# Attention, soft mixture of experts and Mish layer on one core: loads for the last layer moved into rooms that the experts' first weights leave, and one more room

## The chip, the cores and the metric

The kernel runs on one core of one Trainium2 chip (trn2). The metric is the device time of one execution in microseconds. The kernel before takes 679.25 us (median of 3 runs, 678.71 to 683.32).

## The reference, cut to what matters

Three stages follow each other. Attention with rotary positions gives 2304 tokens of 512 features. A soft mixture of 8 experts with 4 slots each mixes the tokens into 32 slots, runs each expert's two weight matrices on its slots, and mixes the results back. The last layer multiplies by `w_in`, applies Mish and multiplies by `w_out`.

```
logits = x @ phi                                  # 2304 x 32
d = softmax of logits over the tokens
slot_input = d.T @ x                              # 32 slots x 512
h = relu(slot_input[e] @ w1[e])                   # 8 experts: 512 -> 1024
slot_out[e] = h @ w2[e]                           # 1024 -> 512
c = softmax of logits over the slots
x = c @ slot_out
h = x @ w_in                                      # 512 -> 2048
g = h * tanh(log1p(exp(h)))                       # Mish
out = g @ w_out                                   # 2048 -> 512
```

## The kernel before, in words

**Attention** (L720 to L746) runs over pairs of heads and takes the first 395 us. Beside it `w_in` is converted and written to a scratch tensor `scr_in` in the chip's memory, and the first expert weights are loaded.

**Rooms.** The experts' weights come in 32 halves of 1 MB (16 of `w1`, 16 of `w2`), each in a *room* of 128 x 2048 words. There are 23 rooms: 14 that are there from the start (5 in pool `ra`, 9 in pool `rd`), 3 in pool `rc` and NRB = 6 in pool `rb` (L768), which opens when attention's buffers are gone. `order` is the list of what still has to come: w1 halves, w2 halves, then four parts of `w_in`. When a half has been multiplied, `used` (L139) hands its room to the next half of the experts, if one is left, and issues its load. If none is left, the room is kept in the list `rooms` when it is one of `ra`. The last four halves of w2 come as 16 quarters of 256 KB.

**Experts.** The first matrices are multiplied at L810 (tile `h_ps`), the second at L843 (`so_ps`). Between the four groups of the second, `combine` (L821) transposes the combine weights of one batch at a time into the tile `ct` (L831, L833).

**Last layer.** It works on units of 256 tokens by 256 hidden features: 72 units in 3 blocks of 24. These steps feed it:

- `load_out(c)` loads rows of `w_out` raw (512 KB) into one of four half-rooms, `outer(c)` makes of them two tiles, a rounded one (`wo_h`) and the rest (`wo_l`). ScalarE scales the raw words (L497, L498) and rounds (L896); VectorE does L503, L504, L505, L509, L510 and the subtraction L897. There are 16 of these, all in the first block.
- `inner(j)` folds the experts' result `s_t` into 256 columns of `w_in`: TensorE `m_wp` (L911), ScalarE copy `wp` (L913), TensorE `m_w` (L915), ScalarE cast L917, VectorE subtraction L918 into `wst`. There are 8, all in the first block.
- `mish(u)` multiplies `wst` with `ct` (TensorE `hp`, L932), ScalarE does Mish (`gg`, L938), a rounded copy `gh` (L940) and the rest `gl` on VectorE (L941). `second(u)` then does 12 matmuls `o_ps` (L957), four units behind.

**What sets the order.** All loads are issued by SyncE's queue in the order of the program; those marked by `keep_in_program_order` stay there. The instructions of TensorE, ScalarE and VectorE are put in order by a scheduler when the kernel is built; on the chip each engine takes its own list from the front. `s_t` (L857) is the experts' result, `so_ps` copied (L853), transposed (`m_sot`, L856) and copied again.

The raw half-rooms and the first two parts of `w_in` are taken from `rooms`, so from rooms of `ra` that the last w2 halves leave (L873 to L878):

```
for i in range(4):
    if i % 2:
        t = rooms[i][0].tile([128, 2048], U32, tag=rooms[i][1], name="raw")
        raws += [t[:, 0:1024], t[:, 1024:2048]]
    else:
        take(*rooms[i])
```

Of the kernel before, what the change touches and what calls it, by code (L numbers as in the profile page):

```python
# [42 lines left out]
def kernel(  # L43
# [13 lines left out]
    nc = tc.nc  # L57
# [6 lines left out]
    R = S - 512  # L64
    SCALE = 1.0 / float(D) ** 0.5
    KDM = DM // 128
    NRA, NRB, NRC = 8, 6, 3


    const = ctx.enter_context(tc.tile_pool(name="const", bufs=1))  # L70
# [22 lines left out]
    ring = ExitStack()  # L93
    ra = ring.enter_context(tc.tile_pool(name="ra", bufs=1, side="right"))
    late = ExitStack()
    rd = late.enter_context(tc.tile_pool(name="rd", bufs=1, side="right"))

    early = ExitStack()
    ae = early.enter_context(tc.tile_pool(name="ae", bufs=1, side="right"))
# [39 lines left out]
    def used(key):  # L139

        room = parts.pop(key)[1]
        if order[0][0] < 3:
            fetch(take(*room))
        elif room[0] is ra:
            rooms.append(room)

    rooms = []
# [612 lines left out]
    h_sb = p4.tile([128, F1], F32, name="h_sb")  # L760
    so_sb = si_t.rearrange("p c x -> p (c x)")[:, 0:DM]
    s_t = p2.tile([128, KDM, NSLOT], F32, name="s_t")
    ct = p2.tile([128, NT], F32R, name="ct")
    nc.gpsimd.memset(si_t, 0.0)
    for t in h_t:
        nc.gpsimd.memset(t, 0.0)
# [51 lines left out]
                used((1, 4 * eg + g, hf))  # L818
    tc.keep_in_program_order(nc.scalar.preload_act_table_set("mish"))

    def combine(b):  # L821

        for t0, nt in ((0, 4), (4, 1)):
            ps = ps_m.tile([128, nt, 128], F32, tag="m", name="m_ct")
            for j in range(nt):
                for o in range(0, 128, 32):
                    nc.tensor.matmul(ps[o:o + 32, j, :], lhsT=c_all[:, b, t0 + j], rhs=ident, start=True, stop=True)
            n = 512 if nt == 4 else R
            src = ps.rearrange("p t n -> p (t n)")[:, 0:n]
            dst = ct[:, b * S + t0 * 128:b * S + t0 * 128 + n]  # L830
            nc.scalar.copy(dst, src)  # L831
            for o in (32, 96):
                nc.vector.tensor_tensor(out=dst[o:o + 32], in0=src[o:o + 32], in1=dst[o:o + 32].bitcast(F32),  # L833
                                        op=ALU.subtract)

    so_ps = ps_m.tile([128, DM], F32, tag="m", name="so_ps")
    for eg in range(2):
# [25 lines left out]
    ps_p = ctx.enter_context(tc.tile_pool(name="ps_p", bufs=2, space=PSUM, reuse_waits="tile"))  # L863
    ps_o = ctx.enter_context(tc.tile_pool(name="ps_o", bufs=6, space=PSUM, reuse_waits="tile"))
    p3 = ctx.enter_context(tc.tile_pool(name="p3", bufs=1, reuse_waits="tile"))
    wo_h = [p3.tile([128, DM], F32R, name=f"wo_h{i}") for i in range(NFC)]
    wo_l = [p3.tile([128, DM], F32R, name=f"wo_l{i}") for i in range(NFC)]
    wst = p3.tile([128, F2], F32R, name="wst")
    p6 = ctx.enter_context(tc.tile_pool(name="p6", bufs=3, reuse_waits="tile"))


    raws = []
    for i in range(4):  # L873
        if i % 2:
            t = rooms[i][0].tile([128, 2048], U32, tag=rooms[i][1], name="raw")
            raws += [t[:, 0:1024], t[:, 1024:2048]]
        else:
            take(*rooms[i])  # L878
    for i in range(2):
        take(p3, f"wi{i}")  # L880

    def load_out(c):

# [4 lines left out]
    def outer(c):  # L888

        t = raws[c % 4]  # L890
        w = p6.tile([128, DM], F32, tag="w", name="w", bufs=2)
        sg = p6.tile([128, DM], U32, tag="sg", name="sg", bufs=2)
        scale_words(t)
        high_word(t, sg, w.bitcast(U32))
        low_word(nc.vector, t, sg, w)
        nc.scalar.copy(wo_h[c], w)  # L896
        nc.vector.tensor_tensor(out=wo_l[c], in0=w, in1=wo_h[c].bitcast(F32), op=ALU.subtract)  # L897

    for x in (0, "i0", 1, 2, 3, "i1"):
        if isinstance(x, int):  # L900
            load_out(x)
        else:
            fetch((3, int(x[1]), 0), behind=True)
# [23 lines left out]
    def mish(u):  # L927
        i, j = units[u]
        hp = ps_p.tile([128, 2, 256], F32, tag="p", name="hp")
        for x in range(2):  # L930
            f = 2 * j + x
            nc.tensor.matmul(hp[:, x, :], lhsT=wst[:, f * 128:(f + 1) * 128], rhs=ct[:, i * 256:(i + 1) * 256],  # L932
                             start=True, stop=True)
        hp = hp.rearrange("p a n -> p (a n)")
        gg = p6.tile([128, 512], F32, tag="gg", name="gg")
        gh = p6.tile([128, 512], F32R, tag="gh", name="gh", bufs=LOOK + 1)
        gl = p6.tile([128, 512], F32R, tag="gl", name="gl", bufs=LOOK + 1)
        nc.scalar.activation(out=gg, in_=hp, func=AF.Mish)  # L938

        (nc.scalar.copy if u < NG * GR else nc.vector.tensor_copy)(gh, gg)  # L940
        nc.vector.tensor_tensor(out=gl, in0=gg, in1=gh.bitcast(F32), op=ALU.subtract)  # L941
        gs[u] = gh, gl
# [3 lines left out]
    def second(u):  # L946
        i, j = units[u]
        gh, gl = gs.pop(u)
        for n in range(2):
# [3 lines left out]
            for x in range(2):  # L953
                f = 2 * j + x
                cols = slice(x * 256 + n * 128, x * 256 + n * 128 + 128)
                for k_, (g_, w_) in enumerate(((gh, wo_h), (gh, wo_l), (gl, wo_h))):
                    nc.tensor.matmul(ps, lhsT=g_[:, cols], rhs=w_[f], start=(j == 0 and x == 0 and k_ == 0),  # L957
                                     stop=(j == NG - 1 and x == 1 and k_ == 2))
            if j == NG - 1:
                ob = p6.tile([128, DM], F32, tag="ob", name="ob", bufs=3)  # L960
# [23 lines left out]
    for u in range(len(units) + LOOK):  # L984
        if u < len(units):
# [3 lines left out]
            if g == 0:  # L989
                if i < 2:  # L990
                    load_out(2 * j + 4 + i)
                if i == 0 and j % 2 == 0 and 2 + j // 2 < NFB:
                    fetch((3, 2 + j // 2, 0), behind=True)
                if j + 1 < NG:
                    if i < 2:
                        outer(2 * j + 2 + i)
                    if i == 1:
                        inner(j + 1)
# [53 lines left out]
```

## Time and profile before

| what | value |
|---|---|
| median of 3 runs | 679.25 us (678.71 to 683.32) |
| the profiled execution | 679.22 us |
| its span in the trace | 677.3 us |
| TensorE matmuls busy | 626.2 us, 92% of the span |
| VectorE, ScalarE, GpSimd busy | 404.9, 332.7, 206.8 us |
| data moved by DMA | 107.32 MB |
| mean granted TensorE clock | 0.982 |

Times in the trace are microseconds from the start of the span. The execution's own time is 1.9 us longer than the span. "Idle before" in a row is how long the engine did nothing ahead of that instruction, with what ended the wait. A busy TensorE row can overlap the next one, since matmuls are pipelined.

### The profile page before, as it was taken

Reading aid. Unit: us, or ns where it says so; the run is one execution under the profiler, and the core shown is the slowest. Engines: PE = TensorE matmul, PEld = TensorE weight load, DVE = VectorE, ACT = ScalarE, POOL = GpSimd, SP = SyncE. Lnnn points to the kernel's source line nnn. Section 1 sums busy time; section 2 is a strip of 40 time slices with the busy share of each in tenths; the row PEclk is TensorE's granted clock in tenths of the full one; section 3 lists DMA queues with packets and bytes.
Section 4 is the critical chain, followed back from the end, with each engine's and each line's share of the span. In section 5 each row is a group of like instructions: output and inputs, shape, how many; then the busy total and the mean of one; then the engine's idle time right before and its main releaser. Section 6 shows DMA issues by size and latency. Waiting matters only on the chain.

```text
span 677.3 us, 11071 instructions
## 1 busy us (share of the span) xinstructions
PE 626.2 (92%) x4002; PEld 461.1 (68%) x4002; DVE 404.9 (60%) x833; ACT 332.7 (49%) x755; POOL 206.8 (31%) x255
## 2 busy tenths in 40 slices
PE   1588899979999999999999998779999999999997
PEld 1565677657677777677677653357787888888885
DVE  6778677784775665656665421599973533343331
ACT  2556766763667656656565301288744321221221
POOL 5659759745675345424300010000000000000000
PEclk9999999998999999999999999969999999999999
DMA  9677689867596775346559579974300300030003
GB/s 265 158 208 186 190 263 270 205 219 199 157 291 183 189 215 130 90 112 172 129 181 315 185 267 379 339 266 164 125 1 0 94 1 0 1 94 0 1 0 94
DMA packets 58454, 107.32 MB, mean 158 GB/s; under 512 B 12704, under 2 KB 25120, under 8 KB 57888
## 3 DMA queue, kind: packets, MB, share of 16 engines
q1 hardware_dynamic: 58400, 106.62, 52.8%
q8 instruction: 32, 0.52, 0.4%
q14 instruction: 22, 0.18, 0.1%
HBM read 69.21 MB, written 8.91 MB: 115 GB/s over the span
## 4 chain that ended last, share of the span: by engine, by line
PE 77%; DMA 7%; DVE 5%; ACT 5%; SPq 2%; issue 2%; POOL 2%; ACTq 0%; DVEq 0%; POOLq 0%
PE o_ps L957 28%; PE m_av L426 14%; PE t L371 8%; PE s L330 5%; PE s L332 4%; PE s L350 3%; DMA w<-in_moe_w_in_dram 3%; PE hp L932 2%; PE so_ps L843 2%; DMA raw<-in_moe_w_out_dram 2%; PE m_lg L452 2%; SPq L185 1%; DMA w<-in_moe_w_dram 1%; PE tk L385 1%; ACT P L364 1%
## 5 line engine op out<-in xcount | busy, mean ns | idle before, releaser
L358 DVE TENSOR_REDUCE nmax<-s 128x1 f32<-128x576 f32 x144 | 108.2, 753 | 66.8 <-PE s L332 38.8
L364 ACT ACTIVATE P<-s,nmax 128x576 f32<-128x576 f32 x144 | 107.3, 745 | 28.2 <-DVE nmax L358 20.5
L957 PE MATMUL o_ps<-wo_h,gh 128*128 128x512 f32 x288 | 114.9, 399 | 0.8 <-ACT gh L940 0.8
L957 PE MATMUL o_ps<-wo_l,gh 128*128 128x512 f32 x288 | 113.9, 396 | 0.0
L957 PE MATMUL o_ps<-wo_h,gl 128*128 128x512 f32 x288 | 108.4, 391 | 0.0
L330 PE MATMUL s<-qk_st 128*128 128x288 f32 x256 | 85.6, 349 | 13.3 <-ACT P L364 7.8
L938 ACT ACTIVATE gg<-hp 128x512 f32<-128x512 f32 x72 | 42.3, 599 | 103.6 <-PE hp L932 100.9
L371 PE MATMUL t<-cs,P 128*128 128x128 f32 x512 | 79.5, 283 | 6.0 <-DVE partl L270 3.3
L407 ACT COPY PT<-t 128x512 f32<-128x512 f32 x93 | 54.2, 586 | 53.4 <-PE t L371 53.0
L371 PEld LDWEIGHTS t<-cs,P 128*128 128x128 f32 x512 | 59.9, 144 | 23.1 <-issue 11.6
L426 PE MATMUL m_av<-PT,w 128*64 128x320 f32 (+1 forms) x384 | 73.1, 421 | 0.9 <-ACT PT L396 0.6
L332 PE MATMUL s<-k_st,qk_st 128*128 128x288 f32 x256 | 73.4, 301 | 0.0
L330 PEld LDWEIGHTS s<-qk_st 128*128 128x128 f32 x256 | 49.7, 194 | 31.0 <-ACT P L364 11.5
L940 DVE CAST gh<-gg 128x512 fp32r<-128x512 f32 x48 | 20.5, 427 | 75.0 <-ACT gg L938 75.0
L228 POOL TENSOR_TENSOR w<-w,cs 128x512 f32<-128x512 f32 x34 | 45.6, 1343 | 61.9 <-PE m_k L282 53.6
L957 PEld LDWEIGHTS o_ps<-wo_h,gh 128*128 128x128 f32 x288 | 54.8, 190 | 13.8 <-ACT gh L940 2.9
L957 PEld LDWEIGHTS o_ps<-wo_h,gl 128*128 128x128 f32 x288 | 54.2, 188 | 11.7 <-DVE sg L509 0.4
L957 PEld LDWEIGHTS o_ps<-wo_l,gh 128*128 128x128 f32 x288 | 54.9, 191 | 9.3
L941 DVE TENSOR_TENSOR gl<-gg,gh 128x512 fp32r<-128x512 f32 x72 | 49.4, 690 | 8.9 <-ACT gh L940 4.4
L332 PEld LDWEIGHTS s<-k_st,qk_st 128*128 128x128 f32 x256 | 49.9, 195 | 0.0
L225 POOL TENSOR_TENSOR w<-w,cs 128x512 f32<-128x512 f32 x34 | 44.5, 1308 | 8.3 <-DMA w<-in_k_dram 3.8
L426 PEld LDWEIGHTS m_av<-PT,w 128*64 128x64 f32 x384 | 26.6, 136 | 22.2 <-issue 9.0
(172 smaller groups left out, 995.6 us busy)
## 6 DMA issues: line engine op xcount, KB each, us to landing
w<-in_moe_w_dram SPq DMA_DIRECT2D x28, 1024.0 KB, 7.6
w<-in_moe_w_in_dram SPq DMA_DIRECT2D x16, 512.0 KB, 6.8
raw<-in_moe_w_out_dram SPq DMA_DIRECT2D x16, 512.0 KB, 4.1
qk_st<-parth SPq DMA_DIRECT2D x46, 144.0 KB, 3.2
qk_st<-partl SPq DMA_DIRECT2D x46, 144.0 KB, 3.2
w<-in_q_dram SPq DMA_DIRECT2D x16, 256.0 KB, 5.5
w<-in_k_dram SPq DMA_DIRECT2D x16, 256.0 KB, 4.7
w<-in_moe_w_dram SPq DMA_DIRECT2D x16, 256.0 KB, 5.6
```

Of the source, the lines that this page charges most:

```text
L225: eng.tensor_tensor(out=tb, in0=src, in1=sin.to_broadcast([128, n, w]), op=ALU.mult)
L228: eng.tensor_tensor(out=dst, in0=sv, in1=cv, op=ALU.mult)
L330: nc.tensor.matmul(s[:, half, 0:288], lhsT=st[:, qc:qc + 128], rhs=st[:, KC + o:KC + o + 288], start=first, stop=False)
L332: nc.tensor.matmul(s[:, half, 0:288], lhsT=st[:, qc:qc + 128], rhs=k2_st[p % 2][:, o:o + 288], start=False, stop=last)
L358: nc.vector.tensor_reduce(out=stat[p][0][:, i:i + 1], in_=s[:, :, 0:288], axis=AX.XY, op=ALU.max, negate=True)
L364: nc.scalar.activation(out=P[p, t][:, h * S:(h + 1) * S].rearrange("p (a b) -> p a b", a=2), in_=s[:, :, 0:288], func=AF.Exp, bias=stat[p] ...
L371: nc.tensor.transpose(ps[:, j, :], P[p, t][:, blk * 128:(blk + 1) * 128], ident)
L407: nc.scalar.copy(dst, src)
L426: nc.tensor.matmul(ps[o:o + 64, :], lhsT=lhsT, rhs=rhs, start=(c == 0), stop=(c == 4))
L938: nc.scalar.activation(out=gg, in_=hp, func=AF.Mish)
L941: nc.vector.tensor_tensor(out=gl, in0=gg, in1=gh.bitcast(F32), op=ALU.subtract)
L957: nc.tensor.matmul(ps, lhsT=g_[:, cols], rhs=w_[f], start=(j == 0 and x == 0 and k_ == 0), stop=(j == NG - 1 and x == 1 and k_ == 2))
```

## The change

It adds one room to `rb` (NRB 6 to 7), so that 24 of the 32 halves have a room from the start and 8 are reloaded instead of 9. It keeps the rooms of `rd` too when no expert weight is left for them. The pool `rd` lives as long as `ra`. The rooms are given out anew, in the order in which they come free: first two for the raw rows of `w_out`, one for part 0 of `w_in`, one for 1792 of the 2304 columns of `ct`, then rooms for the tiles that were `wo_h` and `wo_l` (now `wo[c][0]` and `wo[c][1]`, four tiles in a room) and for parts 1 and 2 of `w_in`. Part 3 gets the room of part 0. `combine` cuts its writes where `ct` is cut. The order of the loads changes: two raw rows ahead of part 0 of `w_in`, and parts 2 and 3 are issued a little later.

```diff
-    NRA, NRB, NRC = 8, 6, 3
+    NRA, NRB, NRC = 8, 7, 3
...
-    rd = late.enter_context(tc.tile_pool(name="rd", bufs=1, side="right"))
+    rd = ring.enter_context(tc.tile_pool(name="rd", bufs=1, side="right"))
...
-        elif room[0] is ra:
+        elif room[0] in (ra, rd):
             rooms.append(room)
...
-    ct = p2.tile([128, NT], F32R, name="ct")
+    CTA = 1792
+    cts = [None, p2.tile([128, NT - CTA], F32R, name="ct1")]
...
+    rt = [room(U32) for _ in range(2)]
+    raws = [t[:, o:o + 1024] for t in rt for o in (0, 1024)]
+    take(*rooms.pop(0))
+    cts[0] = room(F32R)
+    wo = []
+    def wo_room():
+        t = room(F32R)
+        wo.extend((t[:, o:o + DM], t[:, o + DM:o + 2 * DM]) for o in (0, 2 * DM))
+    wo_room()
+    wo_room()
...
-            nc.scalar.copy(dst, src)
-            for o in (32, 96):
-                nc.vector.tensor_tensor(out=dst[o:o + 32], in0=src[o:o + 32], in1=dst[o:o + 32].bitcast(F32),
-                                        op=ALU.subtract)
+            a = b * S + t0 * 128
+            m = min(max(CTA - a, 0), n)
+            for x, y, t, w in ((0, m, 0, a), (m, n, 1, a - CTA)):
+                if x == y:
+                    continue
+                d = cts[t][:, w + x:w + y]
+                nc.scalar.copy(d, src[:, x:y])
+                for o in (32, 96):
+                    nc.vector.tensor_tensor(out=d[o:o + 32], in0=src[o:o + 32, x:y], in1=d[o:o + 32].bitcast(F32),
+                                            op=ALU.subtract)
...
-    wo_h = [p3.tile([128, DM], F32R, name=f"wo_h{i}") for i in range(NFC)]
-    wo_l = [p3.tile([128, DM], F32R, name=f"wo_l{i}") for i in range(NFC)]
...
+    wo_room()
+    take(*rooms.pop(0))
+    wo_room()
+    wo_room()
+    take(*rooms.pop(0))
+    for _ in range(3):
+        wo_room()
...
-    for x in (0, "i0", 1, 2, 3, "i1"):
+    for x in (0, 1, "i0", 2, 3, "i1"):
...
-                if i == 0 and j % 2 == 0 and 2 + j // 2 < NFB:
+                if i == 2 and j in (0, 2):
+                    if j:
+                        take(*parts[3, 0, 0][1])
                     fetch((3, 2 + j // 2, 0), behind=True)
```

On VectorE, from the copy of `s_t` to the first subtraction into `wst`, the kernel before has these rows (`raw` is a raw half-room, `w` and `sg` are work tiles of `outer`, L897 writes `wo_l`):

```order
L503 TENSOR_SCALAR sg<-raw 128x512
L504 SCALAR_TENSOR_TENSOR w<-raw,sg 128x512
L505 TENSOR_SCALAR sg<-w 128x512
L509 TENSOR_TENSOR sg<-sg,raw 128x512
L510 TENSOR_TENSOR w<-w,sg 128x512
L897 TENSOR_TENSOR wo_l_4859<-w,wo_h_4843 128x512
L503 TENSOR_SCALAR sg<-raw 128x512
L504 SCALAR_TENSOR_TENSOR w<-raw,sg 128x512
L503 TENSOR_SCALAR sg<-raw 128x512
L505 TENSOR_SCALAR sg<-w 128x512
L504 SCALAR_TENSOR_TENSOR w<-raw,sg 128x512
L918 TENSOR_TENSOR wst<-m_w,wst 64x256
```

In the changed kernel the same piece of VectorE's list has 15 rows; three of `outer(0)` stand ahead of these twelve (L503, L504, L505), `room` names a raw half-room or a tile of `wo`, L918 is now what L897 was and L939 what L918 was:

```order
L503 TENSOR_SCALAR sg<-room 128x512
L509 TENSOR_TENSOR sg<-sg,room 128x512
L504 SCALAR_TENSOR_TENSOR w<-room,sg 128x512
L510 TENSOR_TENSOR w<-w,sg 128x512
L505 TENSOR_SCALAR sg<-w 128x512
L509 TENSOR_TENSOR sg<-sg,room 128x512
L918 TENSOR_TENSOR room<-w,room 128x512
L510 TENSOR_TENSOR w<-w,sg 128x512
L503 TENSOR_SCALAR sg<-room 128x512
L504 SCALAR_TENSOR_TENSOR w<-room,sg 128x512
L918 TENSOR_TENSOR room<-w,room 128x512
L939 TENSOR_TENSOR wst<-m_w,wst 64x256
```

Ahead of the first subtraction into `wst` stood one whole `outer` and half of another two; now two whole ones and part of a third stand there: 9 instructions of the long kind (L504, L509, L510, L897 and `gl`) instead of 6, and 5 of the short kind (L503, L505) as before. Further down, ahead of the third, fourth and fifth subtraction into `wst`, there are 36, 48 and 63 long ones (before 32, 42 and 58) and 17, 22 and 27 short ones (before 15, 19 and 25); from the seventh on the counts are equal.

On ScalarE, from the first scaling of raw words to the first cast into `wst` (L917 at the end), the kernel before has:

```order
L497 ACTIVATE raw<-raw 128x512
L498 ACTIVATE raw<-raw 128x512
L896 CAST wo_h_4843<-w 128x512
L913 COPY wp<-m_wp 128x256
L497 ACTIVATE raw<-raw 128x512
L498 ACTIVATE raw<-raw 128x512
L497 ACTIVATE raw<-raw 128x512
L498 ACTIVATE raw<-raw 128x512
L917 CAST wst<-m_w 128x256
```

The changed kernel has there (L917 is what L896 was, L934 the copy `wp`, L938 the cast into `wst`):

```order
L497 ACTIVATE room<-room 128x512
L498 ACTIVATE room<-room 128x512
L497 ACTIVATE room<-room 128x512
L498 ACTIVATE room<-room 128x512
L917 CAST room<-w 128x512
L934 COPY wp<-m_wp 128x256
L497 ACTIVATE room<-room 128x512
L498 ACTIVATE room<-room 128x512
L917 CAST room<-w 128x512
L938 CAST wst<-m_w 128x256
```

The scaling of the second raw tile went ahead of the first rounding, and a second rounding stands between the copy `wp` and the cast into `wst`.

On SyncE's queue, behind the last quarter of the experts' weights, the kernel before issues:

```order
L886 DMA raw<-in_moe_w_out_dram 128x1024
L135 DMA w_0_0_4879<-scr_in 128x2048
L886 DMA raw<-in_moe_w_out_dram 128x1024 x3
L135 DMA w_1_0_4881<-scr_in 128x2048
L886 DMA raw<-in_moe_w_out_dram 128x1024
```

The changed kernel issues there:

```order
L907 DMA room<-in_moe_w_out_dram 128x1024 x2
L135 DMA w_0_0_4646<-scr_in 128x2048
L907 DMA room<-in_moe_w_out_dram 128x1024 x2
L135 DMA w_1_0_4856<-scr_in 128x2048
L907 DMA room<-in_moe_w_out_dram 128x1024 x2
```

The order is nearly the same; what differs is the room that each load waits for. The order of attention's instructions on every engine is unchanged.

## Rows read from the trace of the kernel before

**Rows 1.** Stretch, length, busy PE, PEld, DVE, ACT, POOL (count), clock, DMA share, GB/s.

```profile
400.00:404.00 4.00, 4.00 (x44) 1.28 (x40) 0.00 (x0) 0.00 (x0) 0.00 (x0) 1.00 0.05 16
404.00:430.00 26.00, 24.26 (x320) 9.85 (x315) 6.51 (x15) 4.61 (x11) 0.00 (x0) 1.00 1.00 363
434.50:447.10 12.60, 5.58 (x32) 2.84 (x30) 9.99 (x20) 6.20 (x14) 0.00 (x0) 0.62 0.96 383
447.10:451.00 3.90, 3.90 (x13) 3.12 (x10) 3.90 (x8) 2.96 (x6) 0.00 (x0) 0.50 0.73 244
451.00:505.00 54.00, 53.21 (x271) 41.28 (x270) 51.11 (x96) 39.04 (x75) 0.00 (x0) 1.00 0.31 108
```

**Rows 2.** TensorE's waits from 399 to 434.5: us in total, times, longest us.

```profile
PE m_ht L797 <- DVE h_sb L790: 0.9, 1, 0.9
PE m_ht L797 <- ACT h_sb L793: 0.8, 1, 0.8
```

**Rows 3.** The chain that ended last, in order of time: start, us, what.

```profile
431.08 0.98 PE so_ps L843 x8
...
432.41 7.84 DMA raw<-in_moe_w_out_dram
```

**Rows 4.** TensorE in order of time: start, us, what, count, idle before and releaser.

```profile
438.14 1.08 PE L911 MATMUL m_wp<-w,s_t 128*32 128x256 f32 x8 [1.59 <-DVE w L504]
441.07 1.22 PE L915 MATMUL m_w<-wp,cs 128*128 128x256 f32 x2 [1.85 <-ACT wp L913]
444.62 1.22 PE L932 MATMUL hp<-ct,wst 128*128 128x256 f32 x4 [2.33 <-DVE wst L918]
...
447.12 0.80 PE L957 MATMUL o_ps<-wo_h,gh 128*128 128x512 f32 x1
```

**Rows 5.** ScalarE in order of time, same stretch.

```profile
433.25 0.70 ACT L497 ACTIVATE raw<-raw 128x512 f32<-128x512 f32 x1 [1.63 <-DMA raw<-in_moe_w_out_dram]
...
440.13 0.62 ACT L896 CAST wo_h<-w 128x512 fp32r<-128x512 f32 x1 [5.61 <-DVE w L510]
440.65 0.36 ACT L913 COPY wp<-m_wp 128x256 f32<-128x256 f32 x1
```

**Rows 6.** VectorE in order of time, same stretch.

```profile
432.95 0.46 DVE L833 TENSOR_TENSOR ct<-m_ct,ct 32x64 fp32r<-32x64 f32 x2
434.65 0.69 DVE L853 COPY si_t<-so_ps 128x512 f32<-128x512 f32 x1 [1.25 <-PE so_ps L843]
436.58 0.29 DVE L857 COPY s_t<-m_sot 128x128 f32<-128x128 f32 x1 [1.23 <-PE m_sot L856]
...
440.78 0.69 DVE L897 TENSOR_TENSOR wo_l<-w,wo_h 128x512 fp32r<-128x512 f32 x1 [0.74 <-ACT wo_h L896]
...
444.14 0.43 DVE L918 TENSOR_TENSOR wst<-m_w,wst 64x256 fp32r<-64x256 f32 x1
```

**Rows 7.** VectorE from 436.9 to 505 by line: count, busy us, mean ns, idle before.

```profile
L509 DVE TENSOR_TENSOR sg<-sg,raw 128x512 f32<-128x512 f32 x16 | 11.0, 688 | 0.2
...
L503 DVE TENSOR_SCALAR sg<-raw 128x512 uint32<-128x512 uint32 x16 | 6.8, 423 | 0.2 <-ACT raw L497 0.2
```

**Rows 8.** VectorE in order of time: third and fifth subtraction into wst.

```profile
465.30 0.43 DVE L918 TENSOR_TENSOR wst<-m_w,wst 64x256 fp32r<-64x256 f32 x1 [0.37 <-ACT wst L917]
...
485.66 0.43 DVE L918 TENSOR_TENSOR wst<-m_w,wst 64x256 fp32r<-64x256 f32 x1
```

**Rows 9.** TensorE in order of time: the hp matmuls that use those.

```profile
466.07 0.64 PE L932 MATMUL hp<-ct,wst 128*128 128x256 f32 x4
...
487.31 0.65 PE L932 MATMUL hp<-ct,wst 128*128 128x256 f32 x4
```

**Rows 10.** SyncE's queue in order of time: the issue of part 0 of w_in.

```profile
430.15 1.26 SPq L135 DMA_DIRECT2D w<-scr_in  x1
```

**Rows 11.** DMA issues from 431.4 to 433.1: count, KB each, us to landing.

```profile
raw<-in_moe_w_out_dram SPq DMA_DIRECT2D x3, 512.0 KB, 8.6
w<-scr_in SPq DMA_DIRECT2D x1, 1024.0 KB, 7.9
```

More of the change, by code (lines that the diff above doesn't have):

```diff
@@ L819, with room @@
     tc.keep_in_program_order(nc.scalar.preload_act_table_set("mish"))
+    def room(dtype):
+        pool, tag = rooms.pop(0)
+        return pool.tile([128, 2048], dtype, tag=tag, name="room")
+    rt = [room(U32) for _ in range(2)]
[8 more added lines that the diff above has]
+    wo_room()
     def combine(b):
@@ L829, in combine @@
             src = ps.rearrange("p t n -> p (t n)")[:, 0:n]
-            dst = ct[:, b * S + t0 * 128:b * S + t0 * 128 + n]
-            nc.scalar.copy(dst, src)
-            for o in (32, 96):
-                nc.vector.tensor_tensor(out=dst[o:o + 32], in0=src[o:o + 32], in1=dst[o:o + 32].bitcast(F32),
-                                        op=ALU.subtract)
+            a = b * S + t0 * 128
[8 more added lines that the diff above has]
+                                            op=ALU.subtract)
     so_ps = ps_m.tile([128, DM], F32, tag="m", name="so_ps")
@@ L865 @@
     p3 = ctx.enter_context(tc.tile_pool(name="p3", bufs=1, reuse_waits="tile"))
-    wo_h = [p3.tile([128, DM], F32R, name=f"wo_h{i}") for i in range(NFC)]
-    wo_l = [p3.tile([128, DM], F32R, name=f"wo_l{i}") for i in range(NFC)]
     wst = p3.tile([128, F2], F32R, name="wst")
     p6 = ctx.enter_context(tc.tile_pool(name="p6", bufs=3, reuse_waits="tile"))
[L872 to L880, printed above, removed]
+    wo_room()
[5 more added lines that the diff above has]
+        wo_room()
+    assert not rooms
     def load_out(c):
@@ L895, in outer @@
         low_word(nc.vector, t, sg, w)
-        nc.scalar.copy(wo_h[c], w)
-        nc.vector.tensor_tensor(out=wo_l[c], in0=w, in1=wo_h[c].bitcast(F32), op=ALU.subtract)
-    for x in (0, "i0", 1, 2, 3, "i1"):
+        nc.scalar.copy(wo[c][0], w)
+        nc.vector.tensor_tensor(out=wo[c][1], in0=w, in1=wo[c][0].bitcast(F32), op=ALU.subtract)
+    for x in (0, 1, "i0", 2, 3, "i1"):
         if isinstance(x, int):
@@ L931, in mish @@
             f = 2 * j + x
-            nc.tensor.matmul(hp[:, x, :], lhsT=wst[:, f * 128:(f + 1) * 128], rhs=ct[:, i * 256:(i + 1) * 256],
+            nc.tensor.matmul(hp[:, x, :], lhsT=wst[:, f * 128:(f + 1) * 128], rhs=cts[i >= CTA // 256][:, (i * 256) % CTA:(i * 256) % CTA + 256],
                              start=True, stop=True)
@@ L955, in second @@
                 cols = slice(x * 256 + n * 128, x * 256 + n * 128 + 128)
-                for k_, (g_, w_) in enumerate(((gh, wo_h), (gh, wo_l), (gl, wo_h))):
-                    nc.tensor.matmul(ps, lhsT=g_[:, cols], rhs=w_[f], start=(j == 0 and x == 0 and k_ == 0),
+                for k_, (g_, w_) in enumerate(((gh, 0), (gh, 1), (gl, 0))):
+                    nc.tensor.matmul(ps, lhsT=g_[:, cols], rhs=wo[f][w_], start=(j == 0 and x == 0 and k_ == 0),
                                      stop=(j == NG - 1 and x == 1 and k_ == 2))
```

## The prediction, made before the changed kernel ran

> **What bounds the kernel now.** I read the stretches first [rows 1]. From 451 to 505 TensorE is busy 53.21 of 54 us at a granted clock of 1.00, so the first block of the last layer is bound by it. VectorE stands close behind, with 51.11 of the same 54 us: whatever is put ahead of something that TensorE needs is soon felt. The hole is between 434.5, where the experts end, and 447.1, where the first `o_ps` starts: TensorE is busy 5.58 of 12.6 us, and the clock is 0.62 of full. For another 3.9 us it is busy without a break but at 0.50. Ahead of this the experts run without a wait for a load: the only waits of TensorE from 399 to 434.5 are 0.9 and 0.8 us for `h_sb` [rows 2].
>
> The chain view puts 7.84 us of this hole on a load of `w_out` [rows 3], and that is what the change moves ahead. So I looked at who waits for these loads. ScalarE does, 1.63 us, until it scales the first raw tile at 433.25 [rows 5]. But VectorE takes the scaled words only after the copy of `s_t`, which ends at 436.87 [rows 6]; the reader is to see 3 us between the two. The second candidate is part 0 of `w_in`: issued at 430.15 [rows 10] and landed 7.9 us later [rows 11], at 438.05, just ahead of `m_wp` at 438.14 [rows 4]. That is 1.3 us after `s_t`. But the result, there at 439.22, lies until 440.65: ScalarE's list has the rounding L896 ahead of the copy `wp`, and that rounding waited 5.61 us for VectorE's `outer(0)` [rows 5]. So what really ends each wait in the hole is a list: VectorE does `outer(0)` after `s_t`, then ScalarE L896 and `wp`, then TensorE `m_w` at 441.07, then ScalarE and VectorE, with more of `outer` between, and the subtraction into `wst` at 444.14 [rows 6] lets `hp` go at 444.62 [rows 4].
>
> **The change, part by part.** Its own execution took 679.22 us (span 677.3 and 1.9 around it), which is the median of the runs, 679.25, for all purposes.
>
> *One more room.* 1 MB of w2 comes in attention's last load burst instead of as a reload. From 400 to 404 the DMA engines are 0.05 busy, and at the 363 GB/s of the stretch behind [rows 1] 1 MB takes 2.9 us, so it fits into this gap. The eight reloads left then end about 2.9 us earlier than nine did. TensorE never waited for them [rows 2], so I take 0. The other end, a load that meets attention's, would be at most the same 2.9 us.
>
> *Raw rows and part 0 earlier.* With the rooms free long before, they are issued right behind the experts' last quarters. At most this takes away the 1.63 us of ScalarE and the 1.3 us of `m_wp`. Both are covered: the first by `s_t`, the second by ScalarE's list, which still has the rounding ahead of `wp`. I take 0. If the cover were gone (list the other way round), `m_wp` from 436.9 (1.08), `wp` (0.36), `m_w` (1.22), the cast (about as long as `wp`) and the subtraction (0.43) [rows 4 to 6] would let `hp` go at about 440.5, a gain of 4.1 us; that is the other end.
>
> The three raw loads of rows 11 took 8.6 us, with a load of 1 MB among them. [...]
>
> *The lists.* This is the term that counts. On VectorE two `outer` stand ahead of the first subtraction into `wst` where there was one: 9 long instructions instead of 6, 5 short as before. Alone a long one takes 0.688 and a short one 0.423 us [rows 7], but they overlap. Between the end of the first L897 (440.78 + 0.69 = 441.47 [rows 6]) and the fifth subtraction at 485.66 [rows 8] VectorE ran 54 long, 23 short and 4 subtractions of 0.43 us (58 and 25 stand ahead of it, less the 4 and 2 before 441.47): 37.2 + 9.7 + 1.7 = 48.6 us of durations in 44.2 us. So one counts for 0.91 of its duration: 0.63 and 0.385 us.
>
> - First subtraction: 3 x 0.63 = 1.9 us more, less the 0.74 us that VectorE stood idle for L896 [rows 6] and now fills: 1.2 us later.
> - Third: 4 long and 2 short more, 2.5 + 0.8 = 3.3 us; less the idle 0.74 and 0.37 us [rows 6, 8] 2.2 us later. In the kernel before `hp` starts at 466.07 [rows 9], 0.34 us after this subtraction ended (465.30 + 0.43). So TensorE is 1.8 us late.
> - Fifth: 5 long and 2 short more, 3.9 us, less 1.1: 2.8 us later; `hp` came 1.22 us after it (487.31 less 486.09), so 1.6 us late.
> - From the seventh on the counts are equal, so nothing more is added.
>
> These are delays of one list against one clock of TensorE and don't add up: the largest stays, since TensorE, full, has nothing to catch up with. 1.8 us. Bounds: if none of the idle time is filled, 3.3 - 0.34 = 3.0; if TensorE does other units' matmuls meanwhile, 0. I take 1.8, which is worked from the rows of the tightest place.
>
> *The cut of* `ct`. One cast and two subtractions more, of the size that takes 0.46 for two; VectorE idles 1.25 us before it copies `so_ps` [rows 6]. 0; without that cover 0.5 us.
>
> *Other rooms.* The `wo` tiles wait for rooms that the experts left by 434.5, before the first is written. Part 1 of `w_in` waits on SyncE's queue for a room of the third group, as it did; behind it stand raw rows 4 and 5, which wait for VectorE anyway. Parts 2 and 3 of `w_in` are issued later and used by the fifth and seventh `inner`, tens of microseconds on; a part took 7.9 us [rows 11]. 0; without the cover not over 7.9.
>
> Sum: 679.22 + 1.8 = 681.0.
>
> **The rivals.**
>
> 1. *No change*: TensorE's list has enough other work to cover VectorE's. For: 1.22 us of slack at the fifth. Against: 0.34 at the third. 679.2.
> 2. *The hole shrinks*: the loads did decide, as the chain view says. For: 7.84 us on its chain. Against: nobody who waits for it is on the path. The 4.1 us from above: 675.1. [...]
> 3. *Slower by over 1%*: the clock stays down. It was back in the stretch from 451 [rows 1], after 3.90 of 3.90 us of work. If TensorE now waits for VectorE again and again behind its start, at 455 to 460 as the lists suggest, low clock goes on. 3.33 matmuls in a microsecond instead of 5.02 [rows 1]: each 10 us of it cost 3.4. For 20 us: 681.0 + 6.7 = 687.7. It decides if the granted clock from 452 to 472 is below 0.7. Against: that the waits are short, about 1 us each.
> 4. *The early loads hold up the last weights.* Two raw rows and part 0, 2.1 MB, at 363 GB/s 5.8 us if shared evenly, less the 2.9 that the weights gained: 2.9 us later than before. They land by about 430 now, where the DMA's full stretch ends [rows 1], and the last group starts at about 431 [rows 3]: 2 us late, and with the lists 683.
>
> **How the numbers follow.** Forecast 0.55, rivals in order 0.20, 0.10, 0.08, 0.07. A measurement of this kernel can tell about 1%, 6.8 us, from no change. Faster than 672.4 is only the far end of rival 2 with more regained than its price: 0.03. Slower than 686 is most of rival 3 and some of what I can't see: 0.07. Within 1%: 0.90. The range takes in the bounds of the lists, most of rival 2 and of rival 4, and the near part of rival 3: 676 to 685. The forecast's own range is 679.5 to 682.5.
>
> **What would show it.** Right: raw rows and part 0 landed before 434; `m_wp` within 0.2 us of `s_t`, and `wp` still behind a rounding, at 441 or later; first `hp` at 445 to 446 and first `o_ps` near 448; the fifth subtraction at 488 or later; VectorE nearly without idle time from 437 to 490. Wrong: `hp` before 443, a granted clock of 1.00 before 449, or `so_ps` matmuls that wait for a load. Then the loads, not the lists, set the hole.

## The result, and the profile after

The changed kernel took 688.40 us (median of 4 runs, 686.51 to 689.71), the kernel before 680.89 over the 4 runs that belong to it (678.71 to 683.32): a ratio of 1.0107, 95% interval 1.0058 to 1.0157. The forecast was 681.0 with a range to 685, so it is 7.4 us too low. Measured again, both on one chip, it was 686.28 (10 runs) against 681.50 (33 runs): 1.0069, 1.0044 to 1.0093. Two runs of over 2000 us, one of these 33 and one in a series below, are left out of the ratios.

The profiled execution took 689.11 us with a span of 687.2; before it was 679.22 and 677.3. The first thing to see is where the 9.9 us of span begin. The view of one tile gives the first and the last start of the experts' first matmuls (count, ns min/median/max, starts):

```profile
core 0 of [0], span 687.2 us
...
L812 PE MATMUL h_ps<-w,si_t x128: 592/592/617, 403.2 to 418.1; 128*32 128x512 f32 x128
```

They start at 403.2, before at 399.1 (the same view gives 399.1 to 414.1 there): 4.1 us are there before any instruction that the change moves. The experiments show that this part is not the change's. So every stretch below is 4.1 us later than its counterpart in [rows 1]; busy times stand in the order PE, PEld, DVE, ACT, POOL, then clock, DMA share, GB/s:

```profile
408.10:434.10 26.00, 24.26 (x321) 9.89 (x316) 6.51 (x15) 4.62 (x12) 0.00 (x0) 1.00 1.02 377
438.65:451.25 12.60, 4.69 (x30) 2.75 (x30) 11.03 (x22) 5.24 (x11) 0.00 (x0) 0.64 0.64 235
451.25:455.10 3.85, 3.85 (x16) 2.75 (x9) 3.85 (x8) 3.85 (x8) 0.00 (x0) 0.50 0.67 214
455.10:509.10 54.00, 52.14 (x258) 39.28 (x258) 49.65 (x93) 37.38 (x74) 0.00 (x0) 0.99 0.30 104
```

The experts run as before (24.26 of 26 us, and the same waits of 0.9 and 0.8 us as in [rows 2]). In the 12.6 us of the hole TensorE does less (4.69 against 5.58 us), and the hole ends half a us later. In the 54 us behind it TensorE does 258 matmuls where it did 271. Now the chain inside the hole, the counterparts of [rows 4], TensorE in order of time:

```profile
440.96 0.64 PE L932 MATMUL m_wp<-w,s_t 128*32 128x256 f32 x8 [0.38 <-DVE s_t L882]
445.67 1.22 PE L936 MATMUL m_w<-wp,cs 128*128 128x256 f32 x2 [4.07 <-ACT wp L934]
449.21 1.22 PE L953 MATMUL hp<-room,wst 128*128 128x256 f32 x4 [2.32 <-DVE wst L939]
...
451.70 1.65 PE L978 MATMUL o_ps<-room,gh 128*128 128x512 f32 x3
...
493.11 0.71 PE L953 MATMUL hp<-room,wst 128*128 128x256 f32 x4
```

`m_wp` now goes 0.1 us after `s_t` ends: the load is out of the way. What it gained, 1.2 us, is lost at once, since `m_w` waits 4.07 us where it waited 1.85. ScalarE in order of time shows why [rows 5]:

```profile
436.13 0.70 ACT L497 ACTIVATE room<-room 128x512 f32<-128x512 f32 x1
...
444.72 0.62 ACT L917 CAST room<-w 128x512 fp32r<-128x512 f32 x1 [6.16 <-DVE w L510]
445.25 0.37 ACT L934 COPY wp<-m_wp 128x256 f32<-128x256 f32 x1
```

The first raw rows are scaled without a wait for a load, ahead of the end of the experts, and `wp` still stands behind the rounding that VectorE's `outer(0)` releases. VectorE's subtractions into `wst`, first, third and fifth [rows 6, 8]:

```profile
448.72 0.43 DVE L939 TENSOR_TENSOR wst<-m_w,wst 64x256 fp32r<-64x256 f32 x1
...
471.13 0.43 DVE L939 TENSOR_TENSOR wst<-m_w,wst 64x256 fp32r<-64x256 f32 x1 [0.44 <-ACT wst L938]
...
492.53 0.43 DVE L939 TENSOR_TENSOR wst<-m_w,wst 64x256 fp32r<-64x256 f32 x1
```

Less the 4.1 us they are 0.5, 1.7 and 2.8 us later than before; forecast were 1.2, 2.2 and 2.8. So VectorE's delays came about much as foreseen, only the first of them smaller. What TensorE makes of them is not what was foreseen. The forecast let the `hp` of the third subtraction wait for it. Here is that `hp`, with a matmul ahead of it, and the waits of TensorE from 435 to 540 us (us in total, times, longest):

```profile
472.31 1.19 PE L978 MATMUL o_ps<-room,gh 128*128 128x512 f32 x4 [0.47 <-ACT gh L961]
473.34 0.64 PE L953 MATMUL hp<-room,wst 128*128 128x256 f32 x4
...
PE hp L953 <- DVE wst L939: 2.3, 1, 2.3
PE o_ps L978 <- ACT gh L961: 1.8, 3, 1.1
```

The third subtraction ends at 471.56, and the `hp` starts 1.8 us behind it, where it was 0.34 us before. Ahead of it TensorE's list has 12 `o_ps` matmuls where the kernel before has 8: the scheduler has put TensorE's list in another order too, which neither the account of the change nor the forecast looked at. In both kernels only the first `hp` is listed with a wait for a subtraction, 2.3 us. What has grown is the wait of `o_ps` for `gh`, 1.8 us in three waits; before it was 0.8 in two.

The trace holds more. Behind 525 us nothing is left that the lists could change: TensorE does one unit after the other, 2 `hp` and 12 `o_ps` matmuls. The chain view prints the 12 of each unit and, at the end, the last 60 in one row (start, us, what):

```profile
601.89 2.80 PE o_ps L978 x12
...
641.35 2.80 PE o_ps L978 x12
...
668.66 14.02 PE o_ps L978 x60
```

In the kernel before these rows read

```profile
599.43 2.75 PE o_ps L957 x12
...
638.17 2.75 PE o_ps L957 x12
...
659.03 13.64 PE o_ps L957 x60
```

13 units lie between the first two rows in both: 39.46 / 13 = 3.035 us a unit after, 38.74 / 13 = 2.980 before. The clock is 1.00 in both. Every matmul stands some 2% further apart, and no term of the forecast speaks of it.

### The profile page after: what moved, and what is told of

Its sections match the earlier page's. It is cut to its first block, busy times and chain, and to the rows that moved or that the text cites. A ratio compares the mean times of both kernels' runs of the same rounds, so it can differ in the third digit from the quotient of the medians.

```text
span 687.2 us, 11070 instructions
## 1 busy us (share of the span) xinstructions
PE 633.8 (92%) x4002; PEld 464.0 (68%) x4002; DVE 403.4 (59%) x835; ACT 333.1 (48%) x756; POOL 206.2 (30%) x255
## 4 chain that ended last, share of the span: by engine, by line
PE 79%; DVE 7%; ACT 4%; DMA 4%; issue 2%; SPq 2%; POOL 1%; DVEq 0%; ACTq 0%
PE o_ps L978 27%; PE m_av L426 14%; PE t L371 8%; PE s L330 5%; PE s L332 4%; PE s L350 3%; DMA w<-in_moe_w_in_dram 2%; PE hp L953 2%; PE h_ps L812 2%; PE so_ps L868 2%; PE m_lg L452 2%; SPq L314 1%; DMA room<-in_moe_w_out_dram 1%; PE m_k L282 1%; PE tk L385 1%
## 5 line engine op out<-in xcount | busy, mean ns | idle before, releaser
L978 PE MATMUL o_ps<-room,gh 128*128 128x512 f32 x576 | 178.9, 400 | 1.9 <-ACT gh L961 1.8
L978 PEld LDWEIGHTS o_ps<-room,gh 128*128 128x128 f32 x576 | 105.4, 190 | 26.5 <-ACT gh L961 4.8
L978 PE MATMUL o_ps<-room,gl 128*128 128x512 f32 x288 | 109.8, 396 | 0.0
L978 PEld LDWEIGHTS o_ps<-room,gl 128*128 128x128 f32 x288 | 54.1, 188 | 12.8 <-DVE sg L509 0.4
L481 POOL TENSOR_TENSOR c_all<-c_all,tmp 128x64 f32<-128x64 f32 x66 | 18.3, 296 | 70.2 <-DVE tmp L467 69.4
L426 PE MATMUL m_av<-PT,v 128*64 128x256 f32 (+1 forms) x192 | 34.1, 418 | 0.5 <-DVE PT L395 0.5
```

Source lines behind the costliest of these rows:

```text
L426: nc.tensor.matmul(ps[o:o + 64, :], lhsT=lhsT, rhs=rhs, start=(c == 0), stop=(c == 4))
L978: nc.tensor.matmul(ps, lhsT=g_[:, cols], rhs=wo[f][w_], start=(j == 0 and x == 0 and k_ == 0), stop=(j == NG - 1 and x == 1 and k_ == 2))
```

## The experiments

Three things can make a time here: attention, which differs from execution to execution; the lists; and the distance of the matmuls. The second and third lie behind the first `h_ps` matmul. So besides the medians I use T, the span of the profiled execution less the start of its first `h_ps` matmul, 677.3 - 399.1 = 278.2 before and 687.2 - 403.2 = 284.0 after. It repeats to 0.2 us between executions of one kernel, where medians of 10 runs are good to about 0.25%.

### Lists and rooms apart

Unchanged, the two kernels:

> The kernel before, unchanged, on the chip that runs the three others. Three theories for the 7.5 us by which the changed kernel is slower than the kernel before. (A) The lists alone, as forecast: 1.8 us of it are the change, the rest is the difference between chips or executions: here the kernel before would take 683 to 686, with attention ended (first h_ps matmul) at 403 instead of 399 us and 0.232 us between two o_ps matmuls after 520 us instead of 0.227. (B) The rooms: the kernel before stays at 679 to 681, with 399 us and 0.227. (C) Something else of the changed kernel slows attention: the kernel before has its first h_ps matmul at 399, the changed kernel at 403 again.

> The changed kernel, unchanged, on the same chip. (A) 1.8 us, at most 3, above the kernel before in this call. (B) 5.5 to 7.5 us above it: 1.8 from the lists and about 4 from the last layer's steady part, where 864 o_ps matmuls stand 0.005 us further apart. (C) about 4 us of it are there before the first h_ps matmul.

Then the changed kernel with the lists of before, and the kernel before with the lists of the changed one. In both an edge from each instruction of VectorE's and of ScalarE's last layer to the next fixes the order of these two engines:

```diff
+    for name, lst in LISTS.items():
+        own = [i for i in traced[start:] if str(i.engine).endswith(name) and i.outs]
+        nums = [k + int(d) for k, d in enumerate(lst.split())]
...
+        for p, q in zip(nums, nums[1:]):
+            tc.add_manual_dep(own[q], own[p].name,
+                              mybir.DependencyInfo(mybir.DependencyClass.NoSync, mybir.DependencyReason.DATA),
+                              reason="list")
```

TensorE's list is left to the scheduler, and it follows: in the traces TensorE's last layer has the order of the kernel that the lists come from, exactly in the first of the two and but for one `m_wp` in the second. So "the lists" below are those of three engines, and no run parts them.

> The changed kernel with VectorE's and ScalarE's lists of the last layer in the order of the kernel before; rooms and loads stay as changed. (A) and the forecast's term: first hp 10.1 us after so_ps, as before, or up to 4 us less, as the loads are early; the fifth hp group 52.8 us after so_ps ends (54.5 in the changed kernel); 1.6 to 1.8 us faster than the changed kernel. (B) the same 1.6 to 1.8 us, but the kernel stays about 4 us slower than the kernel before, and 0.232 us between two o_ps matmuls. If the lists are worth nothing, as TensorE has other work: the time of the changed kernel.

> The kernel before with VectorE's and ScalarE's lists of the last layer in the order of the changed kernel; rooms and loads stay as before. By the forecast's term 1.6 to 1.8 us slower than the kernel before (bounds 0 and 3.0), with the fifth subtraction into wst 2.8 us later after so_ps. By (B) no more than that, and the distance of the o_ps matmuls stays 0.227 us. If this alone gives 5 us or more, the lists are the whole of the change, and the rooms nothing.

| kernel | median us | ratio to before | T us | us a unit |
|---|---|---|---|---|
| before | 681.01 | 1.0004 (0.9981 to 1.0027) | 278.3 | 2.980 |
| changed | 686.28 | 1.0069 (1.0044 to 1.0093) | 283.8 | 3.035 |
| changed, lists of before | 683.53 | 1.0036 (1.0017 to 1.0056) | 280.9 | 3.035 |
| before, lists of changed | 683.73 | 1.0030 (1.0004 to 1.0055) | 282.0 | 2.980 |

Attention first. This execution of the kernel before has its first `h_ps` matmul even later than the changed kernel had:

```profile
core 0 of [0], span 683.8 us
...
L810 PE MATMUL h_ps<-w,si_t x128: 592/592/617, 405.5 to 420.5; 128*32 128x512 f32 x128
```

So theory (C) falls, and of the 9.9 us between the two first profiles 4.1 are not the change. The medians of the table say the same: the two kernels are 5.3 us apart in them and 5.5 in T, so nothing is left for attention. (A) falls as well, by T and the unit. The lists are worth 2.9 us of T in the changed kernel and 3.7 in the kernel before, where the forecast had 1.8. Why more in the latter stands in its VectorE and ScalarE rows: the new list takes up the second raw tile early, and without the early loads that tile isn't there.

```profile
440.72 0.65 ACT L497 ACTIVATE raw<-raw 128x512 f32<-128x512 f32 x1 [5.04 <-DMA raw<-in_moe_w_out_dram]
...
441.40 0.43 DVE L503 TENSOR_SCALAR sg<-raw 128x512 uint32<-128x512 uint32 x1 [1.72 <-ACT raw L497]
```

The load holds ScalarE for 5.04 us, and ScalarE holds VectorE for 1.72 us in the middle of `outer`. So the lists and the loads belong together: this list needs those loads.

With the lists put back the changed kernel is still 2.6 us above the kernel before in T, with 3.035 us a unit. (B), the rooms, holds. What it is about the rooms is the next question.

### What it is about the rooms

In the rooms four things are new to the matmuls at once. High and low words of two chunks share one tile; `wo` lies higher (the rooms begin at 114,656 bytes of a partition, before it was at 20,256 and up); the short-lived tiles with `gh` and `gl`, which TensorE loads as weights, lie lower (37,664 and up, before 126,752 and up); and the remainders differ: by 512 the addresses of `wo`, `gh` and `gl` all gave 288 before, and now `wo` gives 480 and the others 288. These are the tile addresses of the built programs. One kernel for each; the first two edit the kernel before, the others add one line to the changed kernel:

```diff
 f1 (before)
-    wo_h = [p3.tile([128, DM], F32R, name=f"wo_h{i}") for i in range(NFC)]
-    wo_l = [p3.tile([128, DM], F32R, name=f"wo_l{i}") for i in range(NFC)]
+    wo_t = [p3.tile([128, 4 * DM], F32R, name=f"wo{i}") for i in range(NFC // 2)]
+    wo_h, wo_l = ([wo_t[i // 2][:, o + i % 2 * 2 * DM:o + i % 2 * 2 * DM + DM] for i in range(NFC)] for o in (0, DM))
 f2 (before): the line of p6 stands ahead of the line of p3
 f3, f4 (changed): n = 12288 and n = 48
+    pad = ctx.enter_context(tc.tile_pool(name="pad", bufs=1, reuse_waits="tile")).tile([128, n], F32, name="pad")
     p6 = ctx.enter_context(tc.tile_pool(name="p6", bufs=3, reuse_waits="tile"))
```

> The kernel before with the wo tiles kept where they are as a whole (20 to 86 KB of a partition), but four to a tile, high and low words of two chunks side by side, as the changed kernel's rooms have them. What the earlier four runs left open is why a unit of the steady part (2 hp and 12 o_ps matmuls) takes 3.03 us with the rooms and 2.98 without. If it is the pairing of high and low words: 3.03 us a unit, and 2.4 us more behind the 24th unit. If it is where the tiles lie, or how they stand to the tiles of gh and gl: 2.98 and the time of the kernel before.

> The kernel before with the pool of gh, gl, gg and the other short-lived tiles ahead of the wo tiles: gh and gl at 37 to 57 KB of a partition, as in the changed kernel, instead of 127 to 147; wo at 63 to 129 KB instead of 20 to 86. If the place of the tiles that TensorE loads as weights, or that VectorE and ScalarE write, decides: 3.03 us a unit. If the place of the streamed wo tiles decides and only that above 129 KB is slow, or if the offset of the tiles to one another decides (it stays): 2.98.

> The changed kernel with 48 KB left free ahead of the short-lived tiles, so that gh and gl lie at 87 to 107 KB instead of 38 to 58; wo stays in the rooms above 114 KB. If the place of gh and gl decides: less than 3.03 us a unit, 2.98 at best. If the place of wo, or the offset of the tiles to one another: 3.03.

> The changed kernel with 192 bytes left free ahead of the short-lived tiles, so that gh, gl and the wo rooms have the same remainder of their address by 1024 (992), as they had one (800) in the kernel before; in the changed kernel it is 800 against 992. If the offset to one another decides: 2.98 us a unit, and the kernel about 2.4 us faster than the changed one. If the place of either decides: 3.03.

| kernel | median us | ratio to before | T us | us a unit |
|---|---|---|---|---|
| before, pairs in one tile | 679.99 | 0.9995 (0.9967 to 1.0023) | 278.1 | 2.980 |
| before, short-lived tiles first | 680.99 | 0.9988 (0.9964 to 1.0013) | 278.3 | 2.980 |
| changed, short-lived tiles 48 KB up | 684.38 | 1.0048 (1.0025 to 1.0071) | 280.4 | 3.036 |
| changed, short-lived tiles 192 bytes up | 684.00 | 1.0035 (1.0014 to 1.0056) | 280.4 | 2.980 |

192 bytes give back 3.4 to 3.6 us of T, and the rows of the kernel before are there again:

```profile
599.15 2.74 PE o_ps L979 x12
...
637.89 2.74 PE o_ps L979 x12
...
661.73 13.64 PE o_ps L979 x60
```

Pairing does nothing (2.980 us a unit), and place does nothing where the remainders agree: 2.980 with `wo` above 114 KB as with `wo` below 86. The 48 KB, a multiple of 512 bytes, leave the unit at 3.036, but T falls by 3.5 us, which was not expected: the lists came out otherwise (below).

### The address alone, both causes undone, and a better place

> The kernel before with 192 bytes left free ahead of the short-lived tiles, and nothing else: gh and gl now stand 192 bytes off the wo tiles modulo 1024, as in the changed kernel. If that offset is what the rooms cost: 3.03 us a unit instead of 2.98, 2.4 us more behind the 24th unit, up to 1 us before it, so 2.7 to 3.7 us slower than the kernel before. If it takes the rooms' own place as well: 2.98 and the time of the kernel before.

> The changed kernel with both suspected causes undone: the 192 bytes ahead of the short-lived tiles, and VectorE's and ScalarE's lists of the last layer in the order of the kernel before. Early loads, the seventh room, the cut of the combine weights and the rooms themselves stay. If the two causes are all: from the first h_ps matmul to the end 277.6 to 278.2 us, as in the kernel before (278.1 and 278.2), and its time. If another cost hides in the change: longer by it. If the early loads are worth something by themselves: up to 4 us shorter.

> The changed kernel with 64 bytes left free ahead of the short-lived tiles instead of 192: gh and gl stand 128 bytes off the wo rooms modulo 1024 (0 gave 2.98 us a unit, 192 gave 3.03). If only offsets that differ modulo 128 are dear: 2.98. If the two must agree modulo 256 or more: 3.03, or a value between them.

> The changed kernel with 48 KB and 192 bytes left free ahead of the short-lived tiles: the 48 KB gave other lists, with the first hp 2 us earlier after the experts than in the kernel before, and the 192 bytes give 2.98 us a unit. The sum of the two: from the first h_ps matmul to the end 277.0 to 277.7 us, 0.4 to 1.1 us less than the kernel before, too little for the timed rounds to tell. If the lists of the earlier start hold VectorE back later: 278 to 279.

The first put wo's address less gh's at -192 bytes and measured 2.994 us a unit, T 278.7, median 682.31, 1.0013 (0.9991 to 1.0035): a miss, 3.03 was expected. With 64 bytes instead of 192 (difference 128) it is 3.032, T 283.8. So either the difference is not all, or -192 has another price than +192. Three more kernels look into that, the pad with n = 96, 80 and 128 (like the kernel with 64 bytes one execution each):

> The changed kernel with 384 bytes left free ahead of the short-lived tiles: wo's address less gh's is -192 bytes, as in the kernel before with its 192 bytes. If the difference of the two addresses alone counts: 2.993 us a unit, as there. If the rooms' place counts too: 3.03, or another value.

> The kernel before with 320 bytes left free ahead of the short-lived tiles: wo's address less gh's is -320, which is +192 modulo 512, the changed kernel's difference. If the difference modulo 512 alone counts: 3.03 us a unit and some 3.5 us more from the first h_ps matmul to the end than the 278.1 of the kernel before. If only rooms are dear: 2.98 to 2.993.

> The changed kernel with 512 bytes left free ahead of the short-lived tiles: the difference is -320, the same as the changed kernel's +192 modulo 512. If the difference modulo 512 counts: 3.03 us a unit, as in the changed kernel. If it is taken modulo 1024 or more: another value.

| wo less gh, bytes (modulo 512) | kernel | us a unit | T us |
|---|---|---|---|
| 0 | before; changed + 192 | 2.980; 2.980 | 278.3; 280.4 |
| 128 | changed + 64 | 3.032 | 283.8 |
| 192 | changed; before + 320; changed + 512 | 3.035; 3.047; 3.035 | 283.8; 281.8; 283.9 |
| 320 (-192) | before + 192; changed + 384 | 2.994; 3.005 | 278.7; 281.9 |

The same difference gives nearly the same unit in either kernel, and the kernel before gets the whole cost, 3.5 us of T, without any room. In the traces the lists of VectorE, ScalarE and TensorE are the same with the pad as without.

```profile
600.10 2.80 PE o_ps L958 x12
...
636.66 2.80 PE o_ps L958 x12
...
664.08 14.02 PE o_ps L958 x60
```

At 320 bytes the difference is not all, though. The last 60 matmuls of the kernel before with 192 bytes and of the changed kernel with 384 read

```profile
661.35 13.76 PE o_ps L958 x60
...
664.84 14.01 PE o_ps L979 x60
```

So at one and the same difference the one kernel pays a third of the price that it has at 192 bytes, and the other nearly all of it. What else counts there is open.

What reads or writes the two at once? The last row of each of these fences answers most of it. In the changed kernel these 60 matmuls run from 668.66 us on, and VectorE writes its last `gl` 2 us later (the row after it is a copy of `o_ps` at 675.70):

```profile
669.91 0.69 DVE L962 TENSOR_TENSOR gl<-gg,gh 128x512 fp32r<-128x512 f32 x1
675.70 0.69 DVE L983 COPY ob<-o_ps 128x512 f32<-128x512 f32 x1 [5.10 <-PE o_ps L978]
```

For most of the 14.02 us TensorE is alone with these tiles, and the matmuls are as far apart as before. So the other short-lived tiles, which the pads move too, are hardly the cause. What is left is TensorE against itself: one matmul streams `wo` while the weights of the next are loaded from `gh` or `gl`. In these 14.02 us the matmuls are busy for 14.01 us and the loads of weights, beside them, for 10.88. That is argued from these rows; no run parts the two reads. If the argument holds, the price of the one read beside the other goes with the pair of addresses: a unit takes 2.980 us at a difference of 0 and 3.035 us, 1.8% more, at 192 bytes modulo 512. What on the chip makes that is not shown.

With both causes undone (lists of before, 192 bytes) the changed kernel measures T 277.6, 2.980 us a unit, median 680.02, 0.9982 (0.9953 to 1.0011). So the two causes are all of the loss, and what is left of the change gains 0.6 to 0.7 us of T. The early loads are the likely part of it; they were not tried alone.

The last of the four, 48 KB and 192 bytes, has T 277.2, 1.0 to 1.1 us under the kernel before. By time it can't be told from it: 680.81, 0.9996 (0.9975 to 1.0016). VectorE in order of time shows what the 48 KB do:

```profile
438.62 0.43 DVE L503 TENSOR_SCALAR sg<-room 128x512 uint32<-128x512 uint32 x1
439.08 0.69 DVE L504 SCALAR_TENSOR_TENSOR w<-room,sg 128x512 uint32<-128x512 uint32 x1
439.81 0.69 DVE L878 COPY si_t<-so_ps 128x512 f32<-128x512 f32 x1
```

`outer(0)` begins ahead of the copy of `so_ps`, in the time in which VectorE idled 1.25 us before [rows 6], and fills the wait for `s_t` too. Without the pad its tiles lie on memory that the experts still use: by the addresses of the built programs `w` is at 21,280 to 25,376 bytes, inside the experts' `h_t` (17,696 to 27,936), and with the 48 KB and 192 bytes it begins at 70,624. Now the waits of TensorE in the hole and behind it:

```profile
PE hp L954 <- DVE wst L940: 4.7, 2, 2.9
...
PE m_w L937 <- ACT wp L935: 0.9, 1, 0.9
PE o_ps L979 <- ACT gh L962: 0.6, 2, 0.4
```

`m_w` waits 0.9 us instead of 4.07, and the first `hp` comes 2.0 us earlier than in the kernel before, relative to the experts' start. `hp` pays for it once more, 1.8 us, at the second subtraction. I tried to take that away by putting this one subtraction two places ahead in VectorE's list:

> The changed kernel with 48 KB and 192 bytes left free (277.1 us from the first h_ps matmul to the end), and in VectorE's list the second subtraction into wst two places further ahead. There hp waited 2.0 us for it. If that wait is on the path: up to 1.1 us less, 276.0 to 276.5 us, some 1.5 to 2 us faster than the kernel before, at the edge of what the rounds tell. If VectorE only pays for it later: 277.1.

It failed: T 279.6, 684.20 us, 1.0035 (1.0015 to 1.0055). `hp` waits 3.6 us instead of 4.7, but `o_ps` waits for `gh` more. TensorE's list came out in another order again, so this run does not price the one wait alone.

```profile
PE hp L954 <- DVE wst L940: 3.6, 2, 2.9
PE o_ps L979 <- ACT gh L962: 2.9, 4, 1.0
```

So no version here beats the kernel before by more than the runs can tell.

## Why the prediction was wrong

In the measure T, change by change: the rest of the change, early loads included, -0.6 (both causes undone, 277.6, against 278.2), lists +2.8 (280.4 against 277.6, both with 192 bytes), addresses +3.4 (283.8 against 280.4). Sum 5.6; 283.8 - 278.2 = 5.6.

So of the 7.4 us that the forecast was too low, 3.8 are this sum against its 1.8. Another 1.7 are the start: it set out from 679.22 us, and the four runs of the kernel before have 680.89. The 1.9 left would lie outside T, ahead of the first `h_ps` matmul; in the second series nothing of it is there (5.3 us of medians, 5.5 of T). That it is attention's scatter is likely, not shown.

- **"Other rooms. ... 0; without the cover not over 7.9."** This is the step that failed. It asked when the rooms are free and when loads into them land, and both were right: no matmul waits for a load. It did not ask what changes for the 864 `o_ps` matmuls that read from the rooms. Their operands moved, and with them the difference of two addresses; 3.4 us, nearly twice the forecast's whole loss.
- **"The lists", 1.8, bounds 0 to 3.0.** The term was too small, 2.8, inside the bounds, and its wait was the wrong one. VectorE's delays were worked out rightly. The two kernels with 192 bytes differ in the lists alone; here are their third and fifth subtraction, with the old lists (first `h_ps` matmul at 400.6) and then with the new ones (at 399.6):

```profile
466.02 0.43 DVE L940 TENSOR_TENSOR wst<-m_w,wst 64x256 fp32r<-64x256 f32 x1
486.48 0.43 DVE L940 TENSOR_TENSOR wst<-m_w,wst 64x256 fp32r<-64x256 f32 x1
...
467.17 0.43 DVE L940 TENSOR_TENSOR wst<-m_w,wst 64x256 fp32r<-64x256 f32 x1 [0.23 <-ACT wst L939]
488.44 0.43 DVE L940 TENSOR_TENSOR wst<-m_w,wst 64x256 fp32r<-64x256 f32 x1
```

  Behind the first `h_ps` matmul the new lists make them 2.2 and 3.0 us later, where 2.2 and 2.8 were forecast. (The 2.8 of the changed kernel's fifth have a share of the addresses in them; with 192 bytes it is 2.3 later than in the kernel before.) But "TensorE is 1.8 us late" at the third took TensorE's list as it was, with 0.34 us of slack. That list moved too, the slack became 1.8 us, and behind the first `hp` TensorE waited for no subtraction but for `gh`, which ScalarE's list delays: 1.0 us more. With the 0.5 us at the first `hp` that is 1.5 of the 2.8; where the rest comes together was not tried.
- **"Raw rows and part 0 earlier", 0, other end -4.1.** Right that ScalarE's list and `s_t` cover them: raw rows and part 0 were there before they were wanted, `m_wp` came 0.1 us after `s_t`, `wp` stood behind the rounding. With the lists of before all of the change but the lists and the addresses gains 0.6 us of T; with the changed lists 1.6 (280.4 against 282.0).
- **"One more room", 0.** The experts show no wait for a load, and TensorE's 24.26 us of 26 are the same. "The cut of ct", 0: VectorE idled 1.16 us ahead of the copy of `so_ps`, so it is hidden.
- **Rivals.** The clock did not stay down: 0.99 from 455.1. The hole did not shrink in the changed kernel, but it did in the kernel with 48 KB left free, by 2 us and with `m_w` waiting 0.9, through a list and not through a load; the clock fell there too (with 48 KB and 192 bytes it reads 0.54 from 448 to 452 and 1.00 from 452 to 460). No row here shows a hole in which the clock stayed up, so the price that the chances name for rival 2 has no run behind it. The early loads held up nobody: while the experts run, TensorE waits for `h_sb` alone, 0.9 and 0.8 us.
- **The signs.** First `hp` at 445 to 446 and first `o_ps` near 448 (445.1 and 447.6 less the 4.1), the fifth subtraction at 488.4: all came. So did VectorE without idle time in the 53 us that answer to 437 to 490 (the order is again PE, PEld, DVE),

```profile
441.00:494.00 53.00, 44.57 (x210) 32.51 (x210) 51.28 (x98) 38.43 (x76) 0.00 (x0) 0.87 0.47 161
```

  and the time was still wrong. They tested VectorE's delays, which were foreseen; none looked at what TensorE then waits for, and none at the steady part, where half of the loss lies.

With the address put right the total would have looked right: the changed kernel with 192 bytes is 2.2 us above the kernel before in T, against 1.8. That would have been luck, 2.8 for the lists less 0.6 for the rest.

## What to carry to other kernels

Where a change moves an operand of a long run of matmuls, even by a few hundred bytes, compare the distance of two units in the steady part before and after; it repeats to 0.01 us and shows a loss that no list of waits has. Before you blame the change, try a pad that makes the two operands' addresses equal by 512 bytes; here 192 bytes did it (2.980 us a unit instead of 3.035), and 64 and 512 did nothing (3.032 and 3.035). And measure a stretch from an event that the change can't touch, not the whole span: 4.1 us of the first difference here were attention.

## What the runs showed of the hardware

- The rate of back-to-back matmuls went with the difference of the addresses of weights and streamed operand: 13.64 us for 60 matmuls of 128x512 at a difference of 0, 14.02 at 192 bytes modulo 512, with the clock at 1.00. At 320 bytes the two kernels part, 13.76 in the one and 14.01 in the other. Whole multiples of 512 bytes made no difference (changed kernel 3.035 us a unit, with 512 bytes 3.035, with 48 KB 3.036).
- A shorter hole went with a shorter low clock. The rows are the 30 us that begin 30 us behind the first `h_ps` matmul: the kernel with 48 KB and 192 bytes, the kernel before in its second and its first execution, and the kernel before with the lists of the changed one. The first `hp` starts 43.5, 45.5, 45.5 and 47.8 us behind the first `h_ps` matmul; the mean granted clock is 0.89, 0.83, 0.77 and 0.72. These are means: the first execution of the kernel before, cut into stretches of a microsecond, reads 0.50 in each from 439 to 451 and 1.00 from 452 to 453:

```profile
434.20:464.20 30.00, 21.86 (x172) 13.93 (x165) 27.91 (x58) 21.41 (x43) 0.00 (x0) 0.89 0.75 281
435.50:465.50 30.00, 21.93 (x171) 13.89 (x163) 24.25 (x49) 18.65 (x38) 0.00 (x0) 0.83 0.81 292
429.10:459.10 30.00, 22.98 (x170) 14.48 (x162) 23.96 (x48) 17.97 (x37) 0.00 (x0) 0.77 0.79 295
430.30:460.30 30.00, 19.96 (x150) 12.37 (x142) 23.55 (x48) 16.33 (x33) 0.00 (x0) 0.72 0.76 276
```

- The two executions of the kernel before differ in this clock, 0.77 and 0.83, and have T of 278.2 and 278.3. So that much low clock cost no time here that T shows.
